# Filler matmuls in TensorE's early waits, other transfer times in a list schedule, and a third copy of two attention tiles

## The chip, the cores and the metric

The kernel runs on one core of one Trainium2 chip. The time is device time in microseconds of one execution, from the first to the last instruction and what lies around it; where there are several runs, it is their median.

## What is computed

Attention over 8 batches of 8 heads, 576 positions and 64 values per head, then a mixing layer by Fourier transforms, a normalisation and two matrix products with a ReLU between, in float32; the two weight matrices of 512 x 2048 arrive as float64.

```python
scores = scale * np.matmul(q, k.transpose(0, 1, 3, 2))
mask_plain = (rel >= 0) & (rel < 32)                       # heads 0 to 3
mask_dil = (rel >= 0) & (rel < 128) & (rel % 4 == 0)       # heads 4 to 7
attn = softmax(np.where(masks, scores, -1e9))
x = np.matmul(attn, v)                                     # to (8, 576, 512)
mixed = np.real(np.fft.fft(np.fft.fft(x, axis=1), axis=2))
u = x + mixed
un = (u - mean(u)) / np.sqrt(var(u) + 1e-6)
out = u + np.maximum(un @ w_ch1, 0.0) @ w_ch2
```

## The kernel before

PE is TensorE, DVE is VectorE, ACT is ScalarE, POOL is GpSimd, SP is SyncE.

**How the work is staged.** The attention of a batch is cut into 12 units. A unit (`attend`, L514) is two blocks of 96 queries against 128 keys for two heads: scores on PE (eight matmul records for four products, L523); four masked maxima on DVE that write `pm` and `mx` (L532); four exponentials on ACT in place in `pm` (L538); four transposes on PE into the bank `pt` (L551); a copy on ACT to `ptsb` (L554); four products with the values on PE into the bank `av` (eight records, L558); and the sums, their reciprocals and a product on DVE into `xt` (L566 to L570). `store` (L577) writes `xt` to scratch memory. For each batch, `mix` (L659) reads it back, folds it on POOL, DVE and ACT, and transforms it with float32r matmuls along the sequence (L740, L762) and along the channels (L786, L792); `normalise` writes the rows `u`. `fill` (L1033) runs the first five of the 16 slices of the two weight products for 256 rows at a time, as soon as these rows are there (L888, L904). In parallel `prep` (L839) turns float64 weights into pairs of float32r tiles on ACT, DVE and POOL. When all batches are mixed, the remaining eleven slices follow for nine chunks of 512 rows, one after the other.

**Buffers.** Tiles of a tag are used in turn. `pm` and `ptsb` have two copies each, `mx`, `xt` and the small tiles three. In PSUM the tags `pt` and `av` have one bank each, `mix` and `ff` two, and the scores take halves of two more. The n-th tile of a tag can only be placed once the tile that held its slot is no longer used.

**What sets the order.** No engine's order is written by hand. `Plan.add` (L200) records each operation with its engine, an estimated cost, what it reads and writes, and a priority (smaller is earlier); `at` is the earliest planned time. `Plan.run` (L236) simulates the engines, gives each one that is free the placeable operation of the smallest priority, and emits the operations in that order; on the chip each engine then works through its list strictly in order and waits on semaphores. The simulation has its own model of PE's clock, by which a PE operation costs once or twice its estimate, and its own model of transfers: one pipe for all of them, of a certain width, with a time to start and a time to land (L319 to L321), and at most eight under way for each issuing engine. Attention of batch b has priorities from 12 b, `mix` from 12 (b + 1) + 2, `fill` from 45, the last part from 1000 on.

**The start.** `start` (L458) issues the loads of masks and permutations on SP, clears small tiles on DVE, and requests the Fourier tables on POOL's queue. `blank` (L447, L470) is a row of 512 zeros on one partition; eight transfers copy it to the first row of each scratch array (L480).

Of the kernel before, what the change touches and what calls it, by code (L numbers as in the profile page):

```python
# [19 lines left out]
P = 128  # L20
# [11 lines left out]
NUC = 2  # L32
NH = 6
NLATE = 4
NPE = 1
LO1 = 'DVE'
NFA = 4
# [140 lines left out]
class Plan:  # L178
# [57 lines left out]
    def run(self):  # L236
        ops = self.ops
        busy = {}
        avail, soon = {}, {}
        turn = {t: 0 for t in self.tags}  # L240
        events = [0.0]
        dma = 0.0
        for o in ops:
            busy.setdefault(o.eng, 0.0)
            avail.setdefault(o.eng, [])
            soon.setdefault(o.eng, [])
            if not o.waits:
                heapq.heappush(soon[o.eng], (o.ready, o.num))
                heapq.heappush(events, o.ready)
        order = []  # L250
        used, clock = {}, [0, False]
        lanes = {e: [] for e in busy}

        def place(o, now):
            need = []
            if o.nbytes and len(lanes[o.eng]) >= 8 and lanes[o.eng][-8] > now:
                return False
            for b in o.bufs:
                if b.tag is None or b.ap is not None or b.free_at is not None:
                    continue  # L260
                line, k = self.tags[b.tag], turn[b.tag]
                if line[k] is not b:
                    return False
                if k == 0 and any(x.left or x.free_at > now for x in self.tags.get(self.behind.get(b.tag), ())):
                    return False
                if k >= self.slots[b.tag]:
                    old = line[k - self.slots[b.tag]]
                    if old.left or old.free_at > now:
                        return False
                need.append(b)  # L270
            for b in need:
                turn[b.tag] += 1
                b.free_at = -1.0
            return True

        while events:
            now = heapq.heappop(events)
            while events and events[0] <= now:
                heapq.heappop(events)
            again = True  # L280
            while again:
                again = False
                for eng in busy:
                    if busy[eng] > now:
                        continue
                    while soon[eng] and soon[eng][0][0] <= now:
                        _, n = heapq.heappop(soon[eng])
                        heapq.heappush(avail[eng], (ops[n].prio, n))
                    held, got = [], None
                    while avail[eng]:  # L290
                        e = heapq.heappop(avail[eng])
                        if place(ops[e[1]], now):
                            got = ops[e[1]]
                            break
                        held.append(e)
                        if len(held) > 60:
                            break
                    for e in held:
                        heapq.heappush(avail[eng], e)
                    if got is None:  # L300
                        continue
                    again = True
                    got.start = now
                    order.append(got)
                    cost = got.cost
                    if eng == "PE":
                        win = int(now / WINDOW)
                        while clock[0] < win:
                            load = used.get(clock[0], 0.0) / WINDOW
                            clock[1] = load > 0.45 if clock[1] else load > 0.75  # L310
                            clock[0] += 1
                        cost *= 1 if clock[1] else 2
                        used[win] = used.get(win, 0.0) + min(cost, (win + 1) * WINDOW - now)
                        used[win + 1] = used.get(win + 1, 0.0) + max(0.0, now + cost - (win + 1) * WINDOW)
                    end = now + cost
                    busy[eng] = end
                    heapq.heappush(events, end)
                    done = end
                    if got.nbytes:  # L319
                        dma = max(dma, end + 0.65) + got.nbytes / 3.6e5  # L320
                        done = dma + 1.0  # L321
                        lanes[eng].append(done)
                        heapq.heappush(events, done)
                    for a in got.after:
                        lag = self.OWN[eng] if a.eng == eng else self.LAG[eng]
                        a.ready = max(a.ready, done + lag)
                        a.waits -= 1
                        if not a.waits:
                            heapq.heappush(soon[a.eng], (a.ready, a.num))
                            heapq.heappush(events, a.ready)  # L330
                    for b in got.bufs:
                        b.left -= 1
                        b.free_at = max(b.free_at or 0.0, done + self.LAG[eng])
                        if not b.left:
                            heapq.heappush(events, b.free_at)
        if len(order) != len(ops):
            left = [o for o in ops if o.start is None]
            raise RuntimeError(f"{len(left)} operations can't be placed: {[(o.eng, o.num, o.prio) for o in left[:5]]}")
        self.length = max(busy.values())
        for o in order:  # L340
            o.fn()
# [29 lines left out]
def fused_kernel(ctx: ExitStack, tc, q, k, v, w1, w2, seq, tail, chn, alt, mask, ident, perm, flip, out):  # L371
# [72 lines left out]
    ye = fixed(keep, [P, NSP], F32R, "ye")  # L444
    half = fixed(keep, [P, 1], F32, "half")
    kbs = [fixed(heads, [P, WIN + S], F32, f"kb{i}") for i in range(NKB)]
    blank = fixed(heads, [1, C], F32, "blank")  # L447
    xs = [fixed(keep, [P, C + 1], F32, f"x{i}") for i in range(NX)]
    xtail = [fixed(keep, [P, C + 1], F32, f"xt{i}") for i in range(2)]

# [7 lines left out]
    def start():  # L458
# [8 lines left out]
        zero(half, "DVE", 0.07, lambda: nc.vector.memset(half(), -0.5))  # L467
        for n, t in enumerate(kbs):
            zero(t, "DVE", 0.1, lambda t=t: nc.vector.memset(t()[:, 0:WIN], 0.0), "z", -6.0 + n)
        zero(blank, "DVE", 0.3, lambda: nc.vector.memset(blank(), 0.0))  # L470
        for t in xs + xtail:
            zero(t, "DVE", 0.07, lambda t=t: nc.vector.memset(t()[:, C:C + 1], 0.0), "pad")
        def gaps():
# [4 lines left out]
        zero(ye, "DVE", 0.2, lambda: nc.vector.memset(ye().bitcast(F32), 0.0))  # L478
        for b in range(B):
            dma(lambda b=b: nc.sync.dma_start(  # L480
                out=xsm[b]()[0:1], in_=blank(),
            ), (blank,), ((xsm[b], "zero"),), 12 * b + 6, 2048)
        for i in range(2):
            for m in range(2):
# [29 lines left out]
    def attend(b, dil, j, u, tq, kb, vt, xt, prio):  # L514
# [10 lines left out]
                        rhs=kb()[ps, QB * t:QB * t + KB], start=True, stop=True,  # L525
                    )
        add("PE", 0.75, scores, (tq, kb), (sc,), prio)
        pm = attw("pm", [QB, 4, KB])
        mx = attw("mx", [QB, 4], F32, 3)
        for i in range(4):  # L530
            def masked(i=i):
# [10 lines left out]
        for i in range(4):  # L542
# [7 lines left out]
                    order = ident_sb()[:QB, 1, P - QB:]  # L550
                nc.tensor.transpose(ps()[:, QB * i:QB * i + QB], pm()[:, i], order)  # L551
            add("PE", 0.083, turn, ((pm, i), perm_sb, ident_sb), ((ps, i),), prio)
        pt = attw("ptsb", [P, 4, QB])
        add("ACT", act(4 * QB) - 0.05, lambda: nc.scalar.copy(  # L554
            out=pt().rearrange("p i q -> p (i q)"), in_=ps()[:, :4 * QB]), (ps,), (pt,), prio)
        av = bank("av")
# [591 lines left out]
```

## Time and profile before

| | us |
|---|---|
| median of 3 runs (1163.35 to 1165.95) | 1165.58 |
| the profiled execution | 1167.26 |
| its span, first to last instruction | 1165.5 |

| engine | busy us | share of the span |
|---|---|---|
| PE, matmuls | 1104.5 | 95% |
| PE, weight loads | 928.8 | 80% |
| DVE | 592.2 | 51% |
| ACT | 415.6 | 36% |
| POOL | 298.5 | 26% |

The profile is of one execution. Busy time counts from start to modelled end of the instructions of an engine, so overlapping ends of matmuls are in it; a busy PE is not PE at its peak. A window row gives the busy time of each engine in a stretch of the span, the number of its instructions, the clock that PE was granted as a share of its full 2.4 GHz (0.50 is 1.2 GHz), and what the transfers moved. A wait is idle time of an engine just before an instruction, put down to what released it.

### The profile page before, as it was taken

What the parts mean: (1) busy time and instruction counts of PE and PEld (TensorE: products, weight loads), DVE (VectorE), ACT (ScalarE), POOL (GpSimd) and SP (SyncE); (2) the same over time, 40 slices, a digit from 0 to 9 for tenths busy, and PEclk for the clock granted to TensorE, in tenths of its full rate; (3) what the DMA queues carried; (4) which work ended last, traced back from release to release, by engine and by line L of the source; (5) the groups of instructions that cost most, each with busy time, mean ns of one, the idle gap of its engine ahead of it and who ended that gap; (6) DMA issues with size and microseconds to landing.
All of it is one profiled execution on the core that took longest, in us unless ns stands there. A gap on an engine that the chain in (4) does not pass through costs nothing.

```text
span 1165.5 us, 18027 instructions
## 1 busy us (share of the span) xinstructions
PE 1104.5 (95%) x6472; PEld 928.8 (80%) x6472; DVE 592.2 (51%) x1939; ACT 415.6 (36%) x985; POOL 298.5 (26%) x346
## 2 busy tenths in 40 slices
PE   6888989999999998899988999999999999999998
PEld 5677878888888887799766788888888888888886
DVE  4776777777677779953397414141413222322111
ACT  4565656566455634332243212112121212121210
POOL 1334453524343345610145201001020202020100
PEclk9967899999999999999999999999999999999999
DMA  9753566746465335333263504040313132230101
GB/s 304 227 183 111 178 173 174 222 132 190 124 185 152 110 109 172 126 100 91 89 194 96 145 18 127 19 114 32 108 37 95 51 73 73 55 90 18 56 1 37
DMA packets 100457, 133.76 MB, mean 115 GB/s; under 512 B 8888, under 2 KB 59512, under 8 KB 100368
## 3 DMA queue, kind: packets, MB, share of 16 engines
q1 hardware_dynamic: 96800, 123.70, 35.8%
q0 software_dynamic: 3040, 8.09, 2.4%
q8 instruction: 51, 0.84, 0.3%
q10 hardware_dynamic: 528, 0.82, 0.2%
q14 instruction: 38, 0.31, 0.1%
HBM read 95.82 MB, written 36.75 MB: 114 GB/s over the span
## 4 chain that ended last, share of the span: by engine, by line
PE 59%; DVE 7%; DMA 2%; issue 1%; POOL 1%; ACT 1%; SPq 0%; DVEq 0%; POOLq 0%; ACTq 0%
PE ff L888 25%; PE sc L904 9%; PE mix L904 8%; PE pt L904 4%; PE av L904 4%; PE ff L904 3%; PE pt L888 1%; PE av L558 1%; PE av L888 1%; PE sc L523 1%; PE mix L740 1%; PE mix L786 1%; DMA ut<-in_w_dram 1%; DVE ut L995 1%; DVE wst L865 1%
## 5 line engine op out<-in xcount | busy, mean ns | idle before, releaser
L896 DVE SCALAR_TENSOR_TENSOR hh<-ff,hh 128x512 fp32r<-128x512 f32 x104 | 71.5, 687 | 349.5 <-ACT hh L894 349.5
L894 ACT ACTIVATE hh<-ff 128x512 fp32r<-128x512 f32 x104 | 61.7, 594 | 357.0 <-PE ff L888 356.9
L888 PE MATMUL ff<-utwbb,wb 128*128 128x512 f32 x660 | 160.2, 392 | 2.1 <-ACT utwbb L1012 1.5
L538 ACT ACTIVATE pm<-pm,mx 96x128 f32<-96x128 f32 x384 | 132.8, 394 | 70.1 <-DVE mx L532 64.6
L888 PEld LDWEIGHTS ff<-utwbb,wb 128*128 128x128 f32 x660 | 123.8, 188 | 30.3 <-ACT utwbb L1012 1.9
L888 PE MATMUL ff<-utlate,wb 128*128 128x512 f32 x528 | 127.4, 391 | 0.0
L532 DVE CUSTOM_DVE_ANT_0 pm<-sc,mask_sb 96x128 f32<-96x128 f32 x384 | 94.2, 278 | 44.6 <-PE sc L523 39.8
L888 PEld LDWEIGHTS ff<-utlate,wb 128*128 128x128 f32 x528 | 99.1, 188 | 21.8
L948 POOL DMA_INDIRECT ut<-us,flip_sb x20 | 19.7, 985 | 369.8 <-PE ff L888 219.8
L904 PE MATMUL sc<-wb,hh 128*128 128x512 f32 x396 | 103.8, 394 | 8.0 <-DVE hh L896 5.8
L888 PE MATMUL ff<-ut,wa 128*128 128x256 f32 x720 | 104.4, 293 | 4.3 <-DVE h L896 4.3
L558 PE MATMUL av<-vt,ptsb 128*96 128x65 f32 x768 | 95.2, 273 | 12.7 <-DVE xt L570 10.4
L558 PEld LDWEIGHTS av<-vt,ptsb 128*96 128x96 f32 x768 | 87.1, 187 | 22.7 <-issue 6.7
L904 PE MATMUL mix<-wb,hh 128*128 128x512 f32 x396 | 101.3, 391 | 0.0
L888 PEld LDWEIGHTS ff<-ut,wa 128*128 128x128 f32 x720 | 93.7, 195 | 6.1 <-DVE h L896 5.2
L904 PEld LDWEIGHTS sc<-wb,hh 128*128 128x128 f32 x396 | 73.8, 188 | 27.9 <-DVE hh L896 8.4
L523 PE MATMUL sc<-kb,tq 64*96 64x128 f32 x768 | 77.7, 326 | 14.7 <-DMA tq<-in_q_dram 9.0
L904 PE MATMUL ff<-wa,h 128*128 128x512 f32 x360 | 88.9, 397 | 2.5 <-DVE h L896 2.5
L904 PEld LDWEIGHTS mix<-wb,hh 128*128 128x128 f32 x396 | 74.4, 188 | 16.3
L995 DVE STREAM_TRANSPOSE ut<-ut 128x512 f32<-128x512 f32 (+1 forms) x68 | 65.8, 1017 | 42.1 <-DMA ut<-us 24.5
L904 PEld LDWEIGHTS ff<-wa,h 128*128 128x128 f32 x360 | 66.1, 189 | 17.3 <-DVE h L896 2.9
L523 PEld LDWEIGHTS sc<-kb,tq 64*96 64x96 f32 x768 | 55.6, 187 | 28.2 <-issue 11.4
(143 smaller groups left out, 1657.2 us busy)
## 6 DMA issues: line engine op xcount, KB each, us to landing
vt<-in_v_dram SPq DMA_DIRECT2D x32, 390.0 KB
us<-uc SPq DMA_DIRECT2D x36, 257.0 KB
tq<-in_q_dram SPq DMA_DIRECT2D x32, 288.0 KB
ut<-us SPq DMA_DIRECT2D x36, 256.0 KB
kb<-in_k_dram SPq DMA_DIRECT2D x31, 288.0 KB
ut<-in_w_dram SPq DMA_DIRECT2D x17, 512.0 KB
part<-row SPq DMA_DIRECT2D x32, 256.0 KB
ut<-part SPq DMA_DIRECT2D x32, 256.0 KB
```

What stands on the lines that cost most here:

```text
L523: nc.tensor.matmul(sc()[e][:QB, KB * n:KB * n + KB], lhsT=tq()[ps, QB * t:QB * t + QB], rhs=kb()[ps, QB * t:QB * t + KB], start=True, stop ...
L532: nc.vector.tensor_tensor_reduce(pm()[:, i], sc()[i % 2][:QB, KB * (i // 2):KB * (i // 2) + KB], mask_sb()[:, masks[blocks[i // 2]]], -0.1 ...
L538: add("ACT", 0.295, lambda i=i: nc.scalar.activation(out=pm()[:, i], in_=pm()[:, i], func=AF.Exp, bias=mx()[:, i:i + 1], scale=-1.0), ((mx ...
L558: add("PE", 0.16, lambda i=i: nc.tensor.matmul(av()[:QB, 65 * i:65 * i + 65], lhsT=pt()[:, i], rhs=vt()[:, i % 2, blocks[i // 2]], start=T ...
L740: nc.tensor.matmul(ps()[:, :NSP], lhsT=lt, rhs=tab, start=(m == 0 and n == 0), stop=(m == 2 and n == count - 1),)
L786: nc.tensor.matmul(ps()[:n, :NEP], lhsT=ys[i]()[:, dt, a, rows], rhs=chn_sb[i]()[:, dt, c], start=(dt == 0 and x == 0), stop=(i == 1 and d ...
L888: nc.tensor.matmul(z()[:, :n_tok], lhsT=wf()[:, a, kk], rhs=ut()[:, p, kk], start=(kk == 0 and n == 0), stop=(kk == KT - 1 and n == 2),)
L894: add("ACT", act(n_tok) - 0.05, lambda: nc.scalar.activation(out=h()[:, 0, :n_tok], in_=z()[:, :n_tok], func=AF.Relu), (z,), ((h, 0),), prio)
L896: add("DVE", dve(n_tok), lambda: nc.vector.scalar_tensor_tensor(h()[:, 1, :n_tok], z()[:, :n_tok], 0.0, h()[:, 0, :n_tok].bitcast(F32), op ...
L904: nc.tensor.matmul(acc(), lhsT=h()[:, a, P * s:P * s + P], rhs=wf()[:, p], start=(first and n == 0), stop=(last and n == 2),)
L948: add("POOL", 1.04, lambda: nc.gpsimd.indirect_dma_start(u(), None, us[idx // 4](), bass.IndirectOffsetOnAxis(ap=flip_sb()[:, 4 * kk + idx ...
L995: nc.vector.transpose(out=o[back], in_=x[:, g])
```

## The change

In the planner, a transfer starts 0.9 us after its issue (0.65 before), the pipe moves 270 kB per us (360 before), and the data count as landed 1.6 us after that (1.0 before). `blank` becomes 128 partitions of 512 float32r zeros; its memset stands first among DVE's. A PSUM tile of the tag `ff` and 150 operations on PE are added: each is two matmuls of 256 columns of zeros, with a planned cost of 0.22 us, the priority 900 and the earliest planned times 0, 0.4, 0.8 to 59.6 us. They write a tile that nobody reads. `pm` and `ptsb` get a third copy.

```diff
+NSPIN = 150
...
                     if got.nbytes:
-                        dma = max(dma, end + 0.65) + got.nbytes / 3.6e5
-                        done = dma + 1.0
+                        dma = max(dma, end + 0.9) + got.nbytes / 2.7e5
+                        done = dma + 1.6
...
-    blank = fixed(heads, [1, C], F32, "blank")
+    blank = fixed(heads, [P, C], F32R, "blank")
...
-        zero(blank, "DVE", 0.3, lambda: nc.vector.memset(blank(), 0.0))
+        zero(blank, "DVE", 0.3, lambda: nc.vector.memset(blank().bitcast(F32), 0.0), None, -9.0)
+        spin = bank("ff")
+        for n in range(NSPIN):
+            def turn_over():
+                for _ in range(2):
+                    nc.tensor.matmul(spin()[:, :2 * P], lhsT=blank()[:, :P], rhs=blank()[:, P:3 * P], start=True, stop=True)
+            add("PE", 0.22, turn_over, (blank,), (spin,), 900.0, at=0.4 * n)
...
-                out=xsm[b]()[0:1], in_=blank(),
+                out=xsm[b]()[0:1], in_=blank()[0:1].bitcast(F32),
...
-        pm = attw("pm", [QB, 4, KB])
+        pm = attw("pm", [QB, 4, KB], F32, 3)
...
-        pt = attw("ptsb", [P, 4, QB])
+        pt = attw("ptsb", [P, 4, QB], F32, 3)
```

## Rows read from the trace of the kernel before

**Rows 1.** Stage windows: per engine busy us (instructions), granted clock, DMA share, GB/s.

```profile
0.00:125.00 125.00, 102.07 (x672) 85.76 (x673) 82.42 (x405) 69.99 (x184) 43.70 (x54) 0.85 0.64 205
125.00:570.00 445.00, 422.41 (x3287) 371.48 (x3287) 319.37 (x1271) 224.37 (x595) 168.02 (x222) 0.99 0.49 144
570.00:650.00 80.00, 69.91 (x291) 53.55 (x290) 57.16 (x76) 31.00 (x53) 33.95 (x24) 1.00 0.45 139
650.00:1166.00 516.00, 510.13 (x2229) 417.99 (x2227) 133.20 (x189) 90.22 (x153) 52.83 (x46) 1.00 0.23 64
```

**Rows 2.** Stage windows of the first 122 us, cut where the speed changes.

```profile
0.00:61.00 61.00, 44.92 (x273) 36.51 (x273) 34.89 (x187) 32.21 (x83) 15.14 (x19) 1.00 0.80 255
61.00:68.00 7.00, 5.44 (x52) 4.15 (x50) 4.78 (x33) 5.58 (x16) 0.63 (x1) 1.00 0.81 238
68.00:99.00 31.00, 28.09 (x160) 23.71 (x160) 24.46 (x99) 19.05 (x50) 15.51 (x17) 0.51 0.46 147
99.00:116.00 17.00, 15.47 (x142) 13.85 (x140) 11.49 (x57) 8.90 (x24) 7.71 (x11) 0.99 0.42 129
116.00:122.00 6.00, 5.16 (x29) 4.54 (x30) 5.04 (x28) 3.20 (x10) 4.70 (x7) 0.52 0.53 174
```

**Rows 3.** Timeline of PE: start us, duration us, matmuls merged; around 40, 73, 182 us.

```profile
39.39 1.54 PE L558 MATMUL av<-vt,ptsb 128*96 128x65 f32 x8
41.50 1.17 PE L523 MATMUL sc<-kb,tq 64*96 64x128 f32 x8
...
73.14 1.17 PE L523 MATMUL sc<-kb,tq 64*96 64x128 f32 x8
...
181.36 0.89 PE L558 MATMUL av<-vt,ptsb 128*96 128x65 f32 x8
182.09 0.50 PE L551 MATMUL pt<-perm_sb,pm 96*128 96x96 f32 x4
182.52 0.68 PE L523 MATMUL sc<-kb,tq 64*96 64x128 f32 x8
183.13 0.81 PE L740 MATMUL mix<-tail_sb,eot 128*128 128x290 f32 x4
```

**Rows 4.** Groups of PE's matmuls before 125 us: count, busy us, mean ns, idle before.

```profile
L558 PE MATMUL av<-vt,ptsb 128*96 128x65 f32 x216 | 36.3, 335 | 7.8 <-DVE xt L570 6.7 <-issue 1.1
L523 PE MATMUL sc<-kb,tq 64*96 64x128 f32 x240 | 32.5, 412 | 10.7 <-DMA tq<-in_q_dram 9.0 <-DVE mx L532 1.8
L551 PE MATMUL pt<-ident_sb,pm 96*128 96x96 f32 x67 | 14.9, 338 | 3.2 <-ACT pm L538 2.1 <-ACT ptsb L554 1.0
L551 PE MATMUL pt<-perm_sb,pm 96*128 96x96 f32 x48 | 10.5, 358 | 0.6 <-ACT ptsb L554 0.6
```

**Rows 5.** Timeline of PE: matmuls of 256 columns at 121 and 565 us.

```profile
120.98 2.27 PE L888 MATMUL ff<-ut,wa 128*128 128x256 f32 x9
...
564.95 1.58 PE L888 MATMUL av<-ut,wa 128*128 128x256 f32 x12
566.37 1.58 PE L888 MATMUL pt<-ut,wa 128*128 128x256 f32 x12
```

**Rows 6.** Timeline of DVE: start us, duration us; the memset of the zeros.

```profile
0.99 0.48 DVE L470 MEMSET blank<- 1x512 f32 x1
```

**Rows 7.** Waits of PE before 125 us: total us, times, longest us.

```profile
PE sc L523 <- DMA tq<-in_q_dram: 9.0, 2, 5.4
PE av L558 <- DVE xt L570: 6.7, 7, 2.7
```

**Rows 8.** DMA issues: KB each, median us from issue to landing.

```profile
alt_sb<-in_alt_dram POOLq DMA_DIRECT2D x1, 129.0 KB, 3.2
```

**Rows 9.** Waits of DVE and ACT in the whole run: total us, times, longest.

```profile
DVE pm L532 <- PE pt L551: 2.1, 4, 1.4
...
ACT ptsb L554 <- PE av L558: 4.4, 6, 1.4
```

## Prediction

> **What bounds the kernel now.** I read the stage table first. From 650 us on PE is busy without a break, and from 125 to 570 us it misses 22.6 of 445 us, from 570 to 650 us 10.1 of 80 us [rows 1]. So the end of the kernel is the sum of PE's work and of the time that PE loses. The order of the work matters only through that loss, and the stage with the most loss is the first: PE is called busy for 102.1 of the first 125 us [rows 1], and much of that busy time is slow.
>
> That is seen in the second view, the same stage cut where PE's speed changes, read together with PE's timeline. In the cut, the granted clock stands at 1.00 up to 68 us, at 0.51 from 68 to 99 us, then at 0.99, and once more at 0.52 from 116 to 122 us [rows 2]. The durations contradict its first row. Eight score matmuls take 1.17 us at 41.50 us, exactly what they take at 73.14 us under the half clock, and 0.68 us at 182.52 us; eight `av` matmuls take 1.54 us at 39.39 us and 0.89 us at 181.36 us [rows 3]. So up to about 61 us PE ran at the lower of its two levels (1.2 GHz), whatever the column says, and it did so too in 68 to 99 and 116 to 122 us.
>
> How much is lost? Count what PE had done by 125 us and price it at the upper level. The prices are start to start, so that pipelined ends are not counted: `av` x8 181.36 to 182.09 = 0.73 us, transposes x4 182.09 to 182.52 = 0.43, scores x8 182.52 to 183.13 = 0.61 [rows 3]. By 125 us there were 240 score matmuls (30 groups, 18.3 us), 216 `av` (27 groups, 19.7 us), and 115 transposes (28.75 groups, 12.4 us) [rows 4], so of the 672 matmuls [rows 1] 101 others, nearly all of `mix` and the first `fill`. For these the price of a 256-column matmul, 1.42 us / 12 = 0.118 us (564.95 to 566.37, [rows 5]), raised by a tenth for 258 to 290 columns, gives 0.13 x 101 = 13.1 us. Together 63.5 us of work in 125 us: 61.5 us lost, 22.9 us as idle time and 38.6 us because the same work ran at the low level.
>
> **The change, part by part.**
>
> *Fillers, what they cost.* 150 planned operations of two matmuls each, 256 columns of float32r with a 128-column weight load. The nearest row is the `ff<-ut,wa` matmul of the same shape: 0.118 us at the upper level and 2.27 / 9 = 0.25 us at the lower [rows 5]. A filler is 0.24 us high, 0.50 us low. The first ones run low: from the end of the memset of `blank`, today 1.5 us [rows 6] and about 1.3 us if it goes first, until the first scores at 5.4 us [rows 7] there is room for 8, and I let 15 run low: 15 x 0.50 + 135 x 0.24 = 39.9 us. Bounds: 35.4 us (all high, none of it slow) and 75 us (all low). All of it is PE time in a queue that keeps its order. It costs nothing only as far as it lies in time that PE loses anyway, 61.5 us; so it is a new item of the loss and takes the place of old ones.
>
> *Fillers, what they bring.* Whether zeros lift the clock no row shows. Dense matmuls of the same shape do: nine of them start at 120.98 us at the low level [rows 5], and the row from 122 us on is back at the upper one. I take it that the fillers do the same within some microseconds, and that the planner, which gives PE a filler whenever nothing else can be placed, keeps PE in work until they are used up. They may start at planned times up to 59.6 us, and the last ones then fall into later planned gaps; the `ff` bank that they hold delays the first `fill` at most until they are through. With the clock up, the 38.6 us go, and the 22.9 us of idle time become filler time wherever the plan foresaw the wait.
>
> *What stays lost.* The start until the memset is done: 1.3 us. The second wait for queries, 9.0 - 5.4 = 3.6 us [rows 7]: a filler that stands behind the waiting scores cannot run, and the tables that GpSimd requests at once compete with the load. Waits that the plan doesn't foresee: DVE waits hold `av` for 6.7 us now [rows 7], and with faster scores DVE and ACT are asked for the same work in less time (DVE is busy for 82.4 us of 125 [rows 1]; over 110 us that would be 75%, where 125 to 570 us shows 72%). PE lost 5.1% in that later stage [rows 1]; 5.1% of 115 us is 6 us. And the clock will fall after some of these waits as it did at 68 us, after 7 us in which PE was busy for 5.4 [rows 2]; for two falls, each repaired within 4 us by dense work, at twice the time, I take 3 us. Sum 13.9 us; bounds 5 us (no wait but the first two) and 30 us (today's idle 22.9 us all stay, and 7 us of slow clock).
>
> *The plan's DMA numbers* (0.9 us start, 270 kB per us, 1.6 us landing in place of 0.65, 360 and 1.0). No instruction is added; the order is. By the old numbers the first keys and queries land at 0.5 + 0.65 + 2 x 0.82 + 1.0 = 3.8 us, by the new ones at 0.5 + 0.9 + 2 x 1.09 + 1.6 = 5.2 us; the first scores ran at 5.4 us [rows 7]. The 129 KB load of `alt` took 3.2 us [rows 8]: the old numbers say 2.0, the new 3.0. So the new plan is nearer to this chip, and consumers are queued later, behind work that can run. On PE the gain is bounded by the 22.6 us and 10.1 us that it idles in the later stages [rows 1]; a list schedule that is reordered can also lose there. I take 0, bounds -8 and +8 us, a quarter of that idle time.
>
> *Third copies of `pm` and `ptsb`.* They remove two waits for a free buffer: masked scores behind transposes, 2.1 us on DVE, and the copy of probabilities behind `av`, 4.4 us on ACT, in the whole run [rows 9]. Neither engine is the bound, and behind them the next to be late is the single `pt` and the single `av` bank. I take 1.5 us, about a quarter, bounds 0 and 6.5 us of gain.
>
> *`blank` over 128 partitions, first on DVE.* One memset, off every path: PE's queue now begins with a wait for it, but what stands behind the fillers there is the first scores, which wait for queries until 5.4 us anyway [rows 7]; if it ended later than that, everything would be later by the difference. The eight small stores of zeros wait for it as before.
>
> *Sum.* The loss of the first stage falls from 61.5 to 39.9 + 13.9 = 53.8 us: 7.7 us. With 1.5 us for the third copies that makes 9.2 us. The profiled execution took 1167.3 us (span 1165.5 us and 1.8 us around it), 1.7 us above the median: 1158.1 us on its scale, 1156 us on the scale of the median.
>
> **The rivals.**
>
> *A larger gain (1135 to 1148 us).* The clock rises in the first microseconds and never falls, unforeseen waits cost 5 us, and the reordered later stages give back 8 us: 61.5 - 36 - 5 + 8 = 29 us at most; half of that is likelier. For it: the first stage then looks like 125 to 570 us. Against: the second wait for queries [rows 7] is one for a transfer, and fillers don't speed those.
>
> *Fillers displace work (1166 to 1178 us).* This is the slower side. The plan prices DVE's four masked scores and the rest of a unit lower than it runs, so PE's real waits lie at other places than the planned ones. PE then runs 39.9 us of fillers and still idles, on DVE and ACT, for 22.9 us: 62.8 us, and with some slow clock 66 to 73 us, that is 4 to 11 us more loss than now. It decides from the point at which idle time and slow clock beside the fillers exceed 61.5 - 39.9 = 21.6 us. For it: DVE waits already stop `av` for 6.7 us [rows 7]. Against: nothing behind 125 us, where DVE is as busy and PE loses 5.1% [rows 1], looks like that. The Trainium skill, "TensorE: Matmul & The Clock Gate", Part 1, holds a rule on this side: the cost of the slow start is under 1% of a typical kernel span, here an estimated 11.7 us; by that, a loss of 22.9 + 11.7 = 34.6 us would become one of 53.8 us, and the kernel would take 1185 us. The rows above disagree with it in this kernel, with 38.6 us, unless the engines beside PE set the pace of the first stage, which is this rival.
>
> *No difference (1163 to 1168 us).* The same with about 22 us, or a gain of 9 us that the reordered later stages take back.
>
> *It doesn't do what it says.* Zeros leave the clock down. Then the fillers cost 75 us, and a PE with no room left needs 38.6 + 63.5 + 75 = 177 us for the first stage: some 50 us slower, 1217 us. The trace shows only matmuls of data, so this can't be excluded.
>
> **How the numbers follow.** Forecast (1148 to 1163 us) 0.50; larger gain 0.18; no difference 0.12; displaced work 0.17; clock left down 0.03. About 0.2% (2.3 us) is what a measurement can tell from no change. Faster: 0.50 + 0.18 plus a little of the forecast's neighbours, 0.69; same 0.12; slower 0.19. For 8 in 10 the range goes from 1139 us, where half the larger gain lies, to 1172 us, the middle of displaced work; the forecast's own range is 1148 to 1163 us.
>
> **What would show it.** Right: eight scores at 0.61 us start to start soon after 6 us; the first `ff<-ut,wa` matmul before 113 us (now 120.98 us); stages after 650 us unchanged. Wrong: scores of 1.17 us in 10 to 60 us (clock left down); PE busy without a break, full clock, but the first `fill` as late as now (displaced work); a first stage 10 us shorter whose gain is missing by 570 us (later order).

## Result and profile after

The changed kernel takes 1149.9 us (1149.1 to 1153.6, four runs) beside 1165.8 us for the kernel before: ratio 0.9867, interval 0.9845 to 0.9889. Run again on another occasion it took 1149.6 us beside 1163.7 us (0.9880, 0.9861 to 0.9899). That is 14 to 16 us less; 9.6 us were forecast, with a range of 1139 to 1172 us.

The profile is of the slowest of the four runs (span 1151.8 us). The stage windows of the changed kernel, with the columns of [rows 1]:

```profile
0.00:125.00 125.00, 116.97 (x1074) 106.02 (x1075) 91.52 (x464) 77.29 (x212) 42.70 (x56) 0.99 0.68 218
125.00:570.00 445.00, 422.21 (x3219) 369.98 (x3218) 312.35 (x1216) 220.01 (x575) 170.08 (x224) 0.99 0.49 145
570.00:650.00 80.00, 74.99 (x316) 59.81 (x315) 63.61 (x84) 28.04 (x49) 28.06 (x21) 0.98 0.52 152
650.00:1152.00 502.00, 496.50 (x2169) 406.78 (x2167) 126.76 (x180) 89.16 (x150) 51.75 (x45) 1.00 0.21 59
```

The first 125 us now hold 1074 matmuls instead of 672; 300 of the 402 additional ones are fillers, 102 are work. From 125 to 570 us PE idles 22.8 us, as much as before (22.6); from 570 to 650 us it idles 5.0 us instead of 10.1. The last part of the kernel, from the first `ff<-utwbb` matmul on, begins at 564.1 us instead of 576.4 and takes 587.8 us instead of 589.1.

The same first stage, cut as in [rows 2] and at 6 and 20 us:

```profile
0.00:6.00 6.00, 4.55 (x21) 4.56 (x22) 1.81 (x15) 1.28 (x1) 3.07 (x9) 1.00 0.74 210
6.00:20.00 14.00, 13.44 (x131) 11.80 (x130) 8.36 (x59) 9.21 (x29) 0.00 (x0) 1.00 1.09 382
20.00:61.00 41.00, 39.36 (x377) 35.97 (x376) 28.18 (x145) 25.24 (x70) 7.83 (x9) 1.00 0.71 223
...
68.00:99.00 31.00, 28.42 (x269) 25.52 (x268) 23.78 (x124) 22.84 (x64) 8.73 (x13) 1.00 0.54 171
99.00:116.00 17.00, 15.19 (x127) 13.55 (x126) 15.09 (x63) 8.40 (x24) 13.66 (x17) 0.90 0.44 139
```

From 6 to 99 us PE is busy for 81.2 of the 86 us shown, and the granted clock is 1.00 up to 99 us; behind the first fillers the durations agree with it. PE's timeline, with the columns of [rows 3]:

```profile
1.45 6.25 PE L476 MATMUL ff<-blank 128*128 128x256 f32 x28 [1.45 <-DVE kb L470]
7.63 1.12 PE L530 MATMUL sc<-kb,tq 64*96 64x128 f32 x16
...
13.66 0.68 PE L530 MATMUL sc<-kb,tq 64*96 64x128 f32 x8
14.27 0.89 PE L565 MATMUL av<-vt,ptsb 128*96 128x65 f32 x8
...
36.81 4.32 PE L476 MATMUL ff<-blank 128*128 128x256 f32 x34
40.96 0.81 PE L565 MATMUL av<-vt,ptsb 128*96 128x65 f32 x8
...
117.33 1.57 PE L895 MATMUL ff<-ut,wa 128*128 128x256 f32 x9
```

The 28 first fillers take 6.18 us, 0.22 us each, which is the price of the lower level. The scores behind them are at the upper one: eight of them take 0.68 us at 13.66 us (0.61 start to start, 13.66 to 14.27), where [rows 3] had 1.17 us at 41.50. The 34 fillers at 36.81 us take 4.15 us, 0.122 us each. The first `fill` matmul stands at 117.33 us, before at 120.98 [rows 5]. PE's groups before 125 us, which answer to [rows 4]:

```profile
L476 PE MATMUL ff<-blank 128*128 128x256 f32 x300 | 46.3, 304 | 1.4 <-DVE kb L470 1.4
L565 PE MATMUL av<-vt,ptsb 128*96 128x65 f32 x240 | 26.4, 251 | 1.8 <-DVE xt L577 1.7
L530 PE MATMUL sc<-kb,tq 64*96 64x128 f32 x288 | 24.5, 285 | 2.1 <-DVE mx L539 1.9
L558 PE MATMUL pt<-ident_sb,pm 96*128 96x96 f32 x72 | 11.0, 258 | 2.5 <-ACT ptsb L561 2.4
L558 PE MATMUL pt<-perm_sb,pm 96*128 96x96 f32 x60 | 8.0, 250 | 0.1
```

288 score matmuls instead of 240, 240 `av` instead of 216, 132 transposes instead of 115, and their mean durations are those of the upper level. PE's waits in the same stage, which answer to [rows 7]:

```profile
PE pt L558 <- ACT ptsb L561: 2.4, 3, 1.7
PE sc L530 <- DVE mx L539: 1.9, 6, 0.6
PE av L565 <- DVE xt L577: 1.7, 3, 0.7
PE ff L476 <- DVE kb L470: 1.4, 1, 1.4
```

The two waits for queries (9.0 us) are gone, and the waits of `av` for DVE fell from 6.7 to 1.7 us. All four together are 7.4 us, of 8.0 us that PE idles in this stage.

### The profile page after: what moved, and what is told of

Its sections match the earlier page's. It is cut to its first block, busy times and chain, and to the rows that moved or that the text cites. A ratio compares the mean times of both kernels' runs of the same rounds, so it can differ in the third digit from the quotient of the medians.

```text
span 1151.8 us, 18627 instructions
## 1 busy us (share of the span) xinstructions
PE 1110.7 (96%) x6772; PEld 942.6 (82%) x6772; DVE 594.2 (52%) x1939; ACT 414.5 (36%) x985; POOL 292.6 (25%) x346
## 4 chain that ended last, share of the span: by engine, by line
PE 79%; DVE 14%; issue 2%; DMA 2%; ACT 2%; POOL 1%; SPq 0%; DVEq 0%; ACTq 0%; POOLq 0%
PE ff L895 28%; PE sc L911 9%; PE mix L911 8%; PE ff L911 5%; PE av L565 4%; PE sc L530 4%; PE pt L911 4%; PE av L911 4%; PE ff L476 3%; PE mix L793 2%; DVE pm L539 2%; PE mix L747 2%; PE pt L558 2%; PE pt L895 1%; DVE wst L875 1%
## 5 line engine op out<-in xcount | busy, mean ns | idle before, releaser
L545 ACT ACTIVATE pm<-pm,mx 96x128 f32<-96x128 f32 x384 | 130.4, 394 | 61.1 <-DVE mx L539 59.3
L895 PE MATMUL ff<-ut,wa 128*128 128x256 f32 x720 | 103.9, 292 | 4.5 <-DVE h L903 4.5
L565 PE MATMUL av<-vt,ptsb 128*96 128x65 f32 x768 | 85.3, 251 | 6.1 <-DVE xt L577 3.3
L565 PEld LDWEIGHTS av<-vt,ptsb 128*96 128x96 f32 x768 | 77.8, 167 | 15.0 <-issue 5.4
L911 PEld LDWEIGHTS ff<-wa,h 128*128 128x128 f32 x360 | 65.8, 188 | 14.1
L530 PE MATMUL sc<-kb,tq 64*96 64x128 f32 x768 | 65.3, 288 | 7.7 <-DVE mx L539 7.2
L1002 DVE STREAM_TRANSPOSE ut<-ut 128x512 f32<-128x512 f32 (+1 forms) x68 | 65.8, 1017 | 8.5 <-DMA ut<-us 8.2
L530 PEld LDWEIGHTS sc<-kb,tq 64*96 64x96 f32 x768 | 47.7, 160 | 19.6 <-DVE mx L539 12.7
```

What stands on the lines that cost most here:

```text
L530: nc.tensor.matmul(sc()[e][:QB, KB * n:KB * n + KB], lhsT=tq()[ps, QB * t:QB * t + QB], rhs=kb()[ps, QB * t:QB * t + KB], start=True, stop ...
L545: add("ACT", 0.295, lambda i=i: nc.scalar.activation(out=pm()[:, i], in_=pm()[:, i], func=AF.Exp, bias=mx()[:, i:i + 1], scale=-1.0), ((mx ...
L565: add("PE", 0.16, lambda i=i: nc.tensor.matmul(av()[:QB, 65 * i:65 * i + 65], lhsT=pt()[:, i], rhs=vt()[:, i % 2, blocks[i // 2]], start=T ...
L895: nc.tensor.matmul(z()[:, :n_tok], lhsT=wf()[:, a, kk], rhs=ut()[:, p, kk], start=(kk == 0 and n == 0), stop=(kk == KT - 1 and n == 2),)
L911: nc.tensor.matmul(acc(), lhsT=h()[:, a, P * s:P * s + P], rhs=wf()[:, p], start=(first and n == 0), stop=(last and n == 2),)
L1002: nc.vector.transpose(out=o[back], in_=x[:, g])
```

## Experiments

For each profiled run I counted the matmuls by kind up to a given time and priced them at the upper level with the prices of the prediction (matmuls of 290 columns at 0.133 us, of 258 at 0.1225, the others by columns from 0.118 for 256). "Lost" is the time minus this work; it is good to about 1 us, because a few records can be missing in a trace. The times are medians, the ratios those to the kernel before, measured beside each. The kernel before took 1165.8, 1165.5, 1165.1 and 1163.7 us on the four occasions, so times of different occasions compare to about 2 us only. "Main" is the first matmul of the last part (`ff<-utwbb`). F is the fillers, D the new transfer numbers, C the third copies. The wide `blank` is in every kernel but the one before, and was not run alone.

| kernel | time us | ratio, 95% interval | lost by 125 us | by 200 | lost in 430 to 500 | main starts |
|---|---|---|---|---|---|---|
| before | 1165 | | 62.5 | 73.7 | 12.1 | 576.4 |
| F | 1163.5 | 0.9986 (0.9969 to 1.0003) | 50.7 | 65.8 | 13.9 | 572.6 |
| D | 1164.2 | 0.9983 (0.9965 to 1.0001) | 68.5 | 80.0 | 7.0 | 576.6 |
| C | 1176.2 | 1.0100 (1.0077 to 1.0122) | 63.2 | 77.3 | 10.3 | 585.0 |
| D, C | 1164.1 | 0.9993 (0.9974 to 1.0012) | 65.7 | 75.3 | 7.1 | 574.6 |
| F, C | 1159.0 | 0.9945 (0.9924 to 0.9965) | 48.2 | 64.9 | 12.7 | 566.4 |
| F, D | 1146.5 | 0.9826 (0.9794 to 0.9859) | 51.7 | 61.0 | 9.2 | 559.0 |
| F, D, C (changed) | 1149.9 | 0.9867 (0.9845 to 0.9889) | 53.7 | 60.4 | 8.0 | 564.1 |
| F, D, C again | 1149.6 | 0.9880 (0.9861 to 0.9899) | 53.2 | 59.4 | 8.1 | 558.5 |
| F with 115 | 1154.8 | 0.9921 (0.9901 to 0.9941) | 47.4 | 58.6 | 12.6 | 564.1 |

Two theories stood at the start. By the clock theory the gain is the slow clock and the idle time of the first stage, less the fillers. By the order theory it comes from the planner's new transfer numbers or from the third copies, and the fillers are a cost. The edits are to the changed kernel unless the text names another.

### Fillers alone

```diff
-                        dma = max(dma, end + 0.9) + got.nbytes / 2.7e5
-                        done = dma + 1.6
+                        dma = max(dma, end + 0.65) + got.nbytes / 3.6e5
+                        done = dma + 1.0
...
-        pm = attw("pm", [QB, 4, KB], F32, 3)
+        pm = attw("pm", [QB, 4, KB])
...
-        pt = attw("ptsb", [P, 4, QB], F32, 3)
+        pt = attw("ptsb", [P, 4, QB])
```

> The fillers and the wide row of zeros alone; the old transfer numbers and two copies of pm and ptsb. Clock theory (the gain is the loss of 38.6 us of slow clock and of idle time, less some 40 us of fillers and what stays lost): eight scores at 0.61 us start to start from about 8 us on, time 1150 to 1158 us, most of the 15.8 us. Order theory (the gain comes from the planner's new transfer numbers): 1162 to 1172 us, the clock up but the fillers paid for in full. Buffer theory (third copies): the same as the order theory.

Measured: 1163.5 us, no difference that can be told. The time is the one that the order theory gave, but not in its way: the first stage gained what the clock theory said (lost by 125 us 50.7 instead of 62.5 us), and the gain was gone by the end. The windows of the filler matmuls alone (busy us, count, clock, DMA share, GB/s) show where the fillers stand. The run with fillers alone:

```profile
0.00:60.00 60.00, 22.41 (x130) 0.91 0.84 272
...
100.00:125.00 25.00, 5.02 (x32) 1.00 0.68 205
125.00:150.00 25.00, 5.77 (x38) 1.00 0.53 152
150.00:200.00 50.00, 5.05 (x32) 1.00 0.56 160
```

The changed kernel:

```profile
0.00:60.00 60.00, 31.07 (x200) 1.00 0.80 257
...
100.00:125.00 25.00, 3.29 (x18) 0.93 0.54 168
125.00:150.00 25.00, 0.00 (x0) 1.00 0.56 178
```

With the old transfer numbers 130 filler matmuls run in the first 60 us instead of 200, and the granted clock of that stretch is 0.91. Some 70 come after 125 us; at 0.122 us they are about 8.5 us. From 125 to 200 us the loss is 15.1 us, instead of 6.7 in the changed kernel and 11.2 in the kernel before. How the late fillers cost is not shown in full. The longest late block is twenty matmuls in front of an `av`; in the run's timeline, with a line of DVE:

```profile
157.61 2.63 PE L476 MATMUL ff<-blank 128*128 128x256 f32 x20
...
159.10 0.41 DVE L577 TENSOR_TENSOR xt<-av,rinv 96x256 f32<-96x256 f32 x1
...
160.08 0.81 PE L565 MATMUL av<-vt,ptsb 128*96 128x65 f32 x8
```

This `av` could not have run much earlier: DVE's product into `xt`, which reads the single bank `av`, ended at 159.51 us, 0.6 us before it. So most of this block stands in a real wait.

### No fillers, and the transfer numbers alone

```diff
-NSPIN = 150
+NSPIN = 0
...
-        spin = bank("ff")
+        spin = bank("ff") if NSPIN else None
```

> The changed kernel without its fillers: new transfer numbers and third copies stay. Clock theory: scores of 1.17 us for eight until some 60 us, as in the kernel before, and 1160 to 1168 us. Order or buffer theory: 1148 to 1156 us.

Measured: 1164.1 us; lost by 125 us 65.7. The order and the buffers alone bring nothing, as the clock theory says. The clock is down for longer than expected: eight scores still take 1.17 us at 87.12 us, and 0.68 us at 104.31 us.

```diff
-NSPIN = 150
+NSPIN = 0
...
-        pm = attw("pm", [QB, 4, KB], F32, 3)
+        pm = attw("pm", [QB, 4, KB])
...
-        pt = attw("ptsb", [P, 4, QB], F32, 3)
+        pt = attw("ptsb", [P, 4, QB])
```

> The kernel before with the new transfer numbers alone; no fillers, two copies. Without fillers the clock is down in the first 60 us whatever the order, so I expect no difference beyond the reordering: 1160 to 1169 us. A gain of 10 us or more would say that the order is worth it alone and that the third copies spoiled it in the run without fillers (1164.1 us).

Measured: 1164.2 us. Behind the zero stand two effects. In the first stage the new numbers cost 6.0 us (lost 68.5 instead of 62.5). PE's waits there in this run:

```profile
PE av L565 <- DVE xt L577: 14.9, 9, 5.5
```

`av` waits 14.9 us for DVE instead of 6.7 [rows 7]; why is not shown. PE's idle time in the stage grows by less, from 22.9 to 27.0 us, since the waits for keys and queries are 5.8 us instead of 9.0, and eight scores still take 1.17 us at 110.53 us, so the clock has a share in the loss. And from 430 to 500 us, where DVE prepares the weights of the second part, they give back 5.1 us. Busy time per engine in the kernel before, and below it with the transfer numbers alone:

```profile
430.00:450.00 20.00, 19.10 (x125) 16.97 (x123) 18.44 (x43) 8.25 (x18) 12.22 (x15) 1.00 0.70 218
450.00:500.00 50.00, 42.66 (x261) 37.60 (x262) 45.77 (x88) 21.32 (x46) 29.51 (x31) 0.97 0.40 123
```

```profile
430.00:450.00 20.00, 20.00 (x139) 18.46 (x139) 15.17 (x43) 6.02 (x15) 10.95 (x16) 1.00 0.72 199
450.00:500.00 50.00, 44.73 (x287) 39.29 (x286) 47.89 (x83) 23.32 (x52) 31.49 (x31) 1.00 0.47 143
```

PE is busy for 64.7 of the 70 us instead of 61.8, with DVE as full as before. Fixed times hold different work in the two kernels; at equal work, while the priced work goes from 350 to 400 us, the kernel before loses 11.8 us and this one 6.7. My reading, argued and not shown, is that the two parts need each other: the plan gives PE a filler only where it sees a wait, and the waits that the new numbers put into the first stage cost little when fillers stand in them (51.7 us lost by 125 us, beside 50.7 with fillers and the old numbers).

### The changed kernel with one part taken out

```diff
-        pm = attw("pm", [QB, 4, KB], F32, 3)
+        pm = attw("pm", [QB, 4, KB])
...
-        pt = attw("ptsb", [P, 4, QB], F32, 3)
+        pt = attw("ptsb", [P, 4, QB])
```

> The changed kernel with two copies of pm and ptsb: fillers and new transfer numbers. If the gain is the fillers' together with an early plan that has room for them: all 300 filler matmuls before 125 us, 1148 to 1154 us. If the third copies are the needed partner: more waits of DVE for transposes and of ACT for av, and 1157 to 1164 us as with the fillers alone.

Measured: 1146.5 us, the fastest kernel of this study, ratio 0.9826. All 300 filler matmuls stand before 125 us. The third copies aren't needed.

```diff
-                        dma = max(dma, end + 0.9) + got.nbytes / 2.7e5
-                        done = dma + 1.6
+                        dma = max(dma, end + 0.65) + got.nbytes / 3.6e5
+                        done = dma + 1.0
```

> The changed kernel with the old transfer numbers: fillers and third copies. In the run of the fillers alone 70 of 300 filler matmuls came after 125 us, where PE has other work; if the new transfer numbers are the partner because they leave room early in the plan, this one has the same late fillers and takes 1157 to 1165 us. If the copies are the partner: 1148 to 1154 us.

Measured: 1159.0 us, as expected if the transfer numbers are the partner; 84 filler matmuls come after 125 us, and 16.7 us are lost from there to 200 us. It is 4.5 us faster than the fillers alone although more of its fillers are late, so their number alone does not set the time; what does is open.

### Fewer fillers with the old transfer numbers

```diff
-NSPIN = 150
+NSPIN = 115
```

on the kernel with fillers alone.

> Fillers alone with the old transfer numbers, as in the first run, but 115 in place of 150: about as many as that run had placed by 125 us. If the partner that the new transfer numbers bring is room early in the plan, the 70 late filler matmuls (some 9 us) were what ate the gain: 1152 to 1158 us. If the fillers alone gain nothing for another reason: 1160 to 1166 us as with 150.

Measured: 1154.8 us, 8.7 us less than with 150 (7.6 us by the ratios), about the price of the 70 late filler matmuls. Not all of it is theirs: in the two profiles 3.3 us of it are there by 125 us (47.4 and 50.7 us lost), where both kernels have run 230 filler matmuls, and the granted clock from 0 to 125 us is 1.00 with 115 and 0.96 with 150. The kernel loses less by 200 us than the changed one (58.6 and 60.4) and is 5 us slower: from 430 to 500 us it loses 12.6 us instead of 8.0, the other share of the new transfer numbers (at equal work, from 350 to 400 us of it, 13.3 us instead of 6.7). These two shares, 8.7 us and some 5 us, are about the 14 us between fillers alone and the changed kernel, which has the third copies besides.

### Fillers with fewer columns

```diff
-                    nc.tensor.matmul(spin()[:, :2 * P], lhsT=blank()[:, :P], rhs=blank()[:, P:3 * P], start=True, stop=True)
+                    nc.tensor.matmul(spin()[:, :16], lhsT=blank()[:, :P], rhs=blank()[:, P:P + 16], start=True, stop=True)
```

> The changed kernel with the same plan and the same order on every engine, but each filler matmul has 16 columns in place of 256, so PE gets almost no work from the fillers. It tells what the fillers' work does from what their place in the plan does. Clock theory: PE stays at the low level up to about 60 us, eight scores take 1.17 us, and the first stage loses what it lost before: 1158 to 1172 us. If only the order mattered, and the fillers' work were a cost: the 34 us of fillers go and the time falls to 1125 to 1145 us.

Measured: 1187.8 us (ratio 1.0234, 1.0162 to 1.0306), 38 us above the changed kernel, with the same list of instructions on every engine. The stage windows of this run:

```profile
40.00:50.00 10.00, 10.00 (x59) 8.87 (x59) 6.29 (x37) 5.62 (x18) 0.00 (x0) 0.50 0.42 131
```

PE is full and the clock is at 0.50; 81.1 us are lost by 125 us. What a filler takes is seen in its timeline:

```profile
24.08 1.12 PE L476 MATMUL ff<-blank 128*128 128x16 f32 x8
25.06 0.55 PE L558 MATMUL pt<-ident_sb,pm 96*128 96x96 f32 x4
...
29.95 3.56 PE L476 MATMUL ff<-blank 128*128 128x16 f32 x16
33.44 1.17 PE L530 MATMUL sc<-kb,tq 64*96 64x128 f32 x8
```

At the upper level eight of them take 0.98 us (24.08 to 25.06), 0.122 each, and at the lower level sixteen take 3.49 us, 0.218 each: the same as with 256 columns. So the place and the cost of the fillers are those of the changed kernel at either level, and the only difference is whether the clock rises. It didn't stay up, and the fillers then cost nearly twice. The time is above both ranges, because I had expected narrow fillers to cost almost nothing. Beside the kernel without fillers (1164.1 us) the fillers cost 24 us while the clock is mostly down, and with the clock up 38 us come back: the difference is the 14 us of the change.

```diff
-                    nc.tensor.matmul(spin()[:, :2 * P], lhsT=blank()[:, :P], rhs=blank()[:, P:3 * P], start=True, stop=True)
+                    nc.tensor.matmul(spin()[:, :P], lhsT=blank()[:, :P], rhs=blank()[:, P:2 * P], start=True, stop=True)
```

> The changed kernel, same plan and order, with filler matmuls of 128 columns in place of 256: their work falls from about 36 to about 20 us at the upper level. If 128 columns are still enough to hold the clock up (scores of eight at 0.61 us start to start from 10 us on) the kernel gains up to 12 us more where fillers stood in front of ready work, 1138 to 1148 us; where they only fill time that waits for transfers, nothing, 1146 to 1153 us. If the clock falls as with 16 columns: 1160 to 1190 us.

Measured: three executions of 1156 to 1159 us (ratio 0.9921, 0.9880 to 0.9961) and three of 1178 to 1181 us; the kernel before stayed between 1162 and 1170 us beside them, so the two groups belong to this kernel. What parts them is not shown: the only profile is of the longest execution. Its timeline:

```profile
7.61 2.02 PE L530 MATMUL sc<-kb,tq 64*96 64x128 f32 x16
...
12.61 1.95 PE L476 MATMUL ff<-blank 128*128 128x128 f32 x8
14.36 1.48 PE L565 MATMUL av<-vt,ptsb 128*96 128x65 f32 x8
```

The scores stay at the lower level (16 in 2.02 us), eight fillers take 1.75 us, 0.219 each, and only late, in front of these matmuls at 91 us, does the clock come up:

```profile
91.44 4.22 PE L476 MATMUL ff<-blank 128*128 128x128 f32 x36
95.50 0.84 PE L565 MATMUL av<-vt,ptsb 128*96 128x65 f32 x8
```

36 in 4.06 us, 0.113 each. In neither group do the narrower fillers save anything beside the changed kernel (1149.9 us). That the clock rose earlier in the shorter executions is a guess.

### Half the fillers

```diff
-NSPIN = 150
+NSPIN = 75
```

> The changed kernel with 75 fillers in place of 150. Clock theory with displaced work small: the clock is up from about 8 us, the fillers are used up near 45 us, and after that the clock falls in waits as it did at 68 us in the kernel before; 18 us of fillers less, but 10 to 20 us of slow clock more: 1146 to 1158 us. If the second half of the fillers only displaces work: 1138 to 1146 us.

Measured: 1155.4 us (0.9914, 0.9893 to 0.9935). The stage windows after the last filler at 42 us:

```profile
40.00:50.00 10.00, 8.20 (x67) 7.37 (x67) 5.85 (x24) 3.35 (x8) 1.26 (x1) 0.80 0.30 105
...
70.00:80.00 10.00, 10.00 (x63) 8.10 (x60) 5.26 (x40) 6.11 (x18) 1.41 (x2) 0.50 0.15 44
```

The clock falls at about 46 us and stays at the lower level to beyond 80 us, as in [rows 2]. 62.5 us are lost by 125 us, as much as before, although 18 us of fillers are gone. With all of them the loss there is 8.8 us less and the time 5.5 us less, so the second half of them pays for itself. The profile is of the longest of the four executions (1159.2 us).

### Weights requested later

```diff
-P_QK, P_V, P_TR, P_MIX, P_SPAN, P_W, P_WF, P_FILL, P_FILLT = -8.0, -7.0, -5.0, 2.0, 13.0, 8.0, 8.0, 45.0, 4.0
+P_QK, P_V, P_TR, P_MIX, P_SPAN, P_W, P_WF, P_FILL, P_FILLT = -8.0, -7.0, -5.0, 2.0, 13.0, 20.0, 3.0, 45.0, 4.0
```

on the kernel with fillers and transfer numbers, which was to remove the long blocks of fillers. `P_W` and `P_WF` go from 8 and 8 to 20 and 3. The expectation names the blocks of the changed kernel; in the kernel edited here they are 50 matmuls at 35.00 us and 52 at 57.07 us.

> Fillers and new transfer numbers with two copies, and the five early weight slices requested later (planned priority 20 + 3 f in place of 8 + 8 f), so that the attention's loads of the first batch go ahead of 5 MB of weights. If the long blocks of fillers (34 matmuls near 37 us and 36 near 59 us) stand where the plan waits for transfers, they move and the first batch is done earlier: 1134 to 1144 us. If DVE's later weight preparation then holds the first fill, no difference or a loss: 1146 to 1156 us.

Measured: 1155.7 us (0.9937, 0.9920 to 0.9953), 9 us slower than without it; 59.0 us are lost by 125 us instead of 51.7, and the first `fill` comes at 120.9 us instead of 113.6. The blocks stay:

```profile
32.53 7.44 PE L476 MATMUL ff<-blank 128*128 128x256 f32 x60
39.81 0.81 PE L565 MATMUL av<-vt,ptsb 128*96 128x65 f32 x8
...
41.74 3.83 PE L476 MATMUL ff<-blank 128*128 128x256 f32 x30
45.41 0.81 PE L565 MATMUL av<-vt,ptsb 128*96 128x65 f32 x8
```

60 and 30 matmuls, no fewer than without the edit, so the early weight loads are not what the plan waits for there. In the changed kernel's list of instructions the `av` behind the block of 34 waits for DVE alone, and DVE's last operation before it began at 36.16 us and took 0.41 us, while `av` began at 40.96 us. So `av` was ready for some 4 us behind fillers. What the plan waited for there was not tried.

### Third copies alone

On the kernel before; the wider `blank` is in it too.

```diff
-        pm = attw("pm", [QB, 4, KB])
+        pm = attw("pm", [QB, 4, KB], F32, 3)
...
-        pt = attw("ptsb", [P, 4, QB])
+        pt = attw("ptsb", [P, 4, QB], F32, 3)
```

> The kernel before with third copies of pm and ptsb alone. The waits that they remove were 6.5 us on DVE and ACT in the whole run, none of them seen on PE: 1161 to 1168 us, no difference that can be told.

Measured: 1176.2 us (1.0100, 1.0077 to 1.0122), 11 to 12 us slower than before: a miss. The stage windows:

```profile
30.00:40.00 10.00, 8.69 (x53) 6.96 (x53) 5.39 (x39) 5.91 (x18) 2.01 (x4) 0.51 0.92 267
...
90.00:100.00 10.00, 9.84 (x58) 8.18 (x58) 7.31 (x34) 6.33 (x17) 5.71 (x7) 0.50 0.23 72
```

The clock is at the lower level from 30 to 100 us, as it was for most of that time before, and by 125 us the loss is the same as before (63.2 and 62.5 us). The rest comes later: the last part starts 8.6 us later, of which 2.9 us are lost from 125 to 200 us (14.1 instead of 11.2, with a granted clock of 0.90 instead of 0.98) and 5.1 us from 200 to 430 us (20.5 instead of 15.4), and it takes 590.7 us instead of 589.1. I found no single wait that carries it; beyond that the order is another one, the cause stays open.

### The changed kernel again

Without an edit, beside the kernel before.

> The changed kernel once more, on the same chip as the others of this call, for a closer interval: 1149 to 1152 us, and 2 to 5 us above the same kernel with two copies.

Measured: 1149.6 us, 3.1 us above the kernel with two copies. The two intervals of the ratio (0.9861 to 0.9899 and 0.9794 to 0.9859, from two occasions) only just miss each other; by the ratios of the changed kernel's two measurements the difference is 5 to 6 us.

## Why the prediction was right, point by point

**PE's work and its loss as the measure: right.** The first stage was forecast to lose 53.8 us instead of 61.5. It lost 53.7 and 53.2 us in the two profiles of the changed kernel, instead of 62.5 by the finer prices: 8.8 to 9.3 us gained, 7.7 forecast.

**Slow clock before 61 us, though the column says 1.00: right.** That it costs time is carried by the fillers of 16 columns: same list, same cost of a filler at either level, and 38 us more with the clock mostly down.

**The fillers' cost: right.** 39.9 us were forecast; 28 at 0.22 us and 272 at 0.122 us are 39.4. I had expected 15 low operations (30 matmuls) before the rise; there were about 28 matmuls. The low price of 0.25 us was read from a duration that includes the pipelined end; start to start the same nine matmuls take 2.07 us (the next one starts at 123.05 us), 0.23 each, and the clock came up behind them at 123 us, not from 122 us on. That fillers of zeros raise the clock, which no row showed, is now shown: eight scores take 0.68 us at 13.66 us, and in the same kernel without fillers 1.17 us still at 87 us.

**What stays lost: right in the sum, not in its parts.** 13.9 us were forecast, 53.7 - 39.4 = 14.3 came. The second wait for queries, put at 3.6 us, is gone, since fillers and other work stand before those scores. The unforeseen waits, put at 6 us, are 6.6 (8.0 us of idle time without the 1.4 at the start). One fall of the clock shows, 0.90 over 99 to 116 us, which is 3.4 us at half speed or 1.7 us lost; I had put two falls at 3 us, and no row gave the 4 us of each. The remaining 4.6 us of the 14.3 are in no term, so that the sum agrees is partly luck.

**The transfer numbers: the term that was mis-sized.** I took 0, with bounds of 8 us either way. Alone they are worth nothing, so the 0 would have been right for them. Beside the fillers they are worth 9 us in the changed kernel (1159.0 us without them, 1149.9 with) and 17 us with two copies (1163.5 and 1146.5 us), past the bound. The step that failed is that the sum gave the fillers their gain whatever the plan's numbers: "the last ones then fall into later planned gaps". With the old numbers 70 to 84 filler matmuls come after 125 us, the fillers alone gain nothing that can be told, and 35 operations fewer bring 8.7 us. Of the 14 to 16 us measured the sum had 9.2. By the table the rest lies in two stretches that I had not weighed: from 125 to 200 us the loss fell from 11.2 us to 6.7 and 6.2, and no run isolates the cause; from 430 to 500 us it fell from 12.1 us to 8.0 and 8.1, with the transfer numbers.

**The third copies: wrong in sign.** 1.5 us of gain were forecast, with bounds of 0 and 6.5. They cost 3.1 us in the changed kernel (5 to 6 by the ratios), gained 4.5 us with fillers and old numbers, did nothing with the transfer numbers alone, and cost 11 us alone. The waits that they remove were no measure; what a third copy does here is to give the planner another order. That the whole forecast came near is in part luck too: this term and that of the transfer numbers were off in opposite directions.

**The rival "fillers displace work": it is real, in another kernel.** The fillers alone lose after 125 us what they gained before, and some of it is in the changed kernel, in the block at 37 us. In the changed kernel 14.3 us are lost beside the fillers, below the 21.6 us from which it was to decide. The rival in which zeros leave the clock down, at 1217 us, was priced too high: with the clock mostly down the fillers of 16 columns gave 1187.8 us.

**The Trainium skill's figure.** "TensorE: Matmul & The Clock Gate", Part 1, puts the slow start under 1% of a typical span. These runs disagree with it for this kernel. Of the 38.6 us that the prediction set against it, some 21 lie before 61 us (PE busy for 44.9 us with 23.9 us of priced work), 1.8% of the time; the rest belongs to the later falls at 68 and 116 us. And with the same list of instructions and the clock down for most of the first 125 us, the time is 38 us longer, 3.3%.

**A sign that failed.** The first `fill` was to come before 113 us and came at 117.3. With the old transfer numbers and fillers it comes at 103.9 us. By 125 us both of these kernels have run 36 groups of scores, beside 30 in the kernel before; the changed one has run 70 more filler matmuls by then. For the end the later `fill` didn't matter: the kernel with the earlier one took 1163.5 us.

## What to carry to other kernels

Where one engine bounds a long list schedule, count its lost time stage by stage, with the fast price of its work; a part of a change is worth what it takes from that sum, and the sum shows at once where a gain is given back. Read the clock from durations of the same instruction, and fill known waits of the matrix engine with spare matmuls, but try their number: here 70 too many cost up to 8.7 us, and with half as many the clock fell at 46 us and stayed down beyond 80 us. Before leaving parts of a change together, take each one out: the planner's numbers were worthless alone and 9 of the 14 to 16 us together with the fillers, and the kernel without the third copies, at 1146.5 us, beats the changed one by about 3 us.

## What the runs showed of the hardware that I had not expected

A matmul with a new 128-column weight load of float32r costs the same with 16, 128 and 256 columns: 0.122, 0.113 and 0.122 us start to start at the upper level, 0.218, 0.219 and 0.22 at the lower. With 256 columns of zeros the granted clock first rose by 8 us in all eight profiles of kernels that have them, and fell again later; with 128 it rose at 90 us in the one profile; and with 16 it stood at 0.50 from 30 to 70 us in the one profile, though PE was busy without a gap there.
